# First weight sums: their loads moved to ScalarE's queue, four of five blocks' sums moved to GpSimd

## The chip, the cores and the metric

The kernel runs on one core of one Trainium2 chip. The metric is the device time of one execution in microseconds; less is better. A core has five engines, each with an instruction queue of its own that is worked through in order: TensorE (PE in the profile, with its weight loads as PEld), VectorE (DVE), ScalarE (ACT), GpSimd (POOL) and SyncE (SP). An engine's queue also issues the DMAs that are written for it; an issue that has to wait holds up what stands behind it in that queue.

## The reference

Attention with a routing mask, then a feed-forward layer with hard-swish, all in fp32:

```python
batch, n_heads, seq, head_dim = (4, 8, 768, 64);  n_clusters = 16
n_tokens, d_model, d_ff = (3072, 512, 2048)
q_assign = np.argmax(einsum('bhsd,hcd->bhsc', q_n, c_n), axis=-1)   # k_assign likewise
mask = q_assign[:, :, :, None] == k_assign[:, :, None, :]
scores = np.where(mask, scale * q @ k.T, -1e9)
attn = softmax(scores);  attn_out = attn @ v
x = attn_out.transpose(0, 2, 1, 3).reshape(B * S, H * D)
h = x @ w_in
g = h * np.clip(h + 3.0, 0.0, 6.0) / 6.0
return g @ w_out
```

## The kernel before

**Stages.** The order of the instructions is written out by hand; nothing is reordered. Heads are taken in pairs, 16 pairs in all, four to a batch.

- *Attention* (to about 240 us): the first 8 pairs, with all keys for every query. The loop runs over n, 12 steps to a pair: scores on TensorE (L400), their exponentials on ScalarE (L423), a running sum `acc` of the exponentials on GpSimd (`key_sums`, L430 and L433), the product with v on TensorE (L443). At the end of each half of a pair TensorE sums `acc` over the partitions (`pd`, L467), and VectorE takes the reciprocal (L473). Between the steps VectorE decodes the weights, which come as 8-byte numbers (L232 to L259).
- *The late pairs* (to about 790 us): the other 8 pairs are sorted by cluster first. GpSimd scatters the rows of q, k and v into DRAM by indirect DMAs (`scatter`, L1034), SyncE loads the sorted rows (`piece`, `vs`), TensorE transposes them (L919), only a band of the scores is computed, and GpSimd gathers the result back (`gather`, L1050). These steps stand in a plan of points; after each point one half of an item of the feed-forward layer follows.
- *The end*: the feed-forward layer alone.

**The feed-forward layer** is done in 12 blocks of 256 tokens, `(b, m)`. A block has 8 up items (`up`, one for two chunks of d_ff) and then 7 down items (`down`). Up items are numbered through as `u`: items 0 to 7 are block 0, 8 to 15 block 1, up to 95. Block 0 does plain products (`ph`, L607); its up items stand in the attention loop at n = 60, 64, 70, 72, 82, 84, 90 and 94. From block 1 on each item is a product of 2x2 blocks with 7 in place of 8 multiplications (`halved`), into two PSUM tiles: `uX`, whose first matmul reads `tx`, and `uY`, which reads `tx` too. `tx` holds three sums of blocks of w_in for this item, 384 KB.

**The sums.** `kept_sums(i)` makes the three sums of item i of a block by three subtractions of 128x256 (L551) and stores them in a DRAM tensor `td` (L559). During attention this is done for five of the eight i, at the up items of block 0 that `sooner` names, ahead of the item's matmuls; the other three, and a last subtraction in w_in itself, follow in the down items of block 0.

**The loads.** `first_sums(u + 2)` loads an item's sums back from `td` two items ahead, in `begin` of item u (L548). `tx` has three buffers, so the buffer of item u+2 is the one that item u-1 has read. The order in an item from block 1 on is: `begin` runs the lift of the item before on ScalarE (`raise_gates`, L499), then the load of `tx`, then the `uX` matmuls, a copy of a quarter of `uX` on ScalarE (L677) and two sums on VectorE; `end` runs `uY`, three sums on VectorE (L670), the clip of the item before (L502) and, every second item, four sums for the down products (`gated_sums`, L649, on GpSimd or VectorE).

All plain loads and stores are issued by SyncE, in the order of the program, except the load of the centroids and one store of each of the last four blocks, which ScalarE issues.

Of the kernel before, what the change touches and what calls it, by code (L numbers as in the profile page):

```python
# [12 lines left out]
ALU = mybir.AluOpType  # L13
# [106 lines left out]
def fast_path(ctx, tc, ok, q, k, v, centroids, moe_w_in, moe_w_out, out):  # L120
# [3 lines left out]
    nc = tc.nc  # L124
# [373 lines left out]
    def lift(r, h):  # L498
        nc.scalar.activation(out=r, in_=h, func=ACT.Relu, bias=half_c, scale=1.0 / 6.0)  # L499

    def clip(g, r, h):
        nc.vector.scalar_tensor_tensor(out=g, in0=r, scalar=1.0, in1=h, op0=ALU.min, op1=ALU.mult)  # L502
# [25 lines left out]
    td = dram.tile([P, HF, 3, HK, P], F32, name="td")  # L528
# [3 lines left out]
    def load_block():  # L532
        if waiting and st["free"]:
            b, m = waiting.pop(0)
            st["free"] = False
            xb = st["xb", b, m] = xbp.tile([P, NKT, 2 * P], F32, name="xb")
            nc.sync.dma_start(xb, st["xd", b][:, :, 2 * m * P : 2 * (m + 1) * P])

    def wi(s, t, i):
        f = t * HF + i  # L540
        return w_in_sb[:, s * HK : (s + 1) * HK, f * P : (f + 1) * P]

    def first_sums(u):

        blk, i = divmod(u, HF)
        if ("tx", u) not in st and 0 < blk < B * NHC:
            tx = st["tx", u] = txp.tile([P, 3, HK, P], F32, name="tx")
            nc.sync.dma_start(tx, td[:, i])  # L548

    def subtract(out_, in0, in1):  # L550
        nc.vector.tensor_tensor(out=out_, in0=in0, in1=in1, op=ALU.subtract)  # L551

    def kept_sums(i):

        tx = txp.tile([P, 3, HK, P], F32, name="tx")
        t1, t2, t4 = (tx[:, k] for k in range(3))
        for sums in ((t1, wi(0, 1, i), wi(0, 0, i)), (t2, wi(1, 1, i), t1), (t4, wi(1, 0, i), t2)):
            subtract(*sums)
        nc.sync.dma_start(td[:, i], tx)  # L559
        if i < 2:  # L560
            st["tx", HF + i] = tx
        st["kept"].add(i)

    def make_first_sums(i):
        if i not in st["kept"]:
            kept_sums(i)
        subtract(wi(0, 1, i), wi(1, 1, i), wi(0, 1, i))

    def token_sums(b, m):

# [15 lines left out]
    def ffn_items(b):  # L586
        def up(m, i):
            u = (b * NHC + m) * HF + i
            g = g_sb[:, 0:4, i]
            got = {}  # L590

            def begin():
                raise_gates()
                load_block()
                if u >= HF:
                    first_sums(u + 2)
                    halved(b, m, u, i, got)

            def end():
                if u < HF:  # L600
                    for other in sooner.get(u, ()):
                        kept_sums(other)
                    ph = psum_m.tile([P, 512], F32, name="ph", tag="m")
                    for t in range(2):
                        f = t * HF + i
                        for kt in range(NKT):
                            nc.tensor.matmul(  # L607
                                ph[:, t * HC : (t + 1) * HC], lhsT=w_in_sb[:, kt, f * P : (f + 1) * P],
                                rhs=st["xb", b, m][:, kt], start=(kt == 0), stop=(kt == NKT - 1),
                            )  # L610
                    ph = ph.rearrange("p (k c) -> p k c", k=4)
                    lift(g, ph)
                    if i < HF - 1:
                        clip(g, g, ph)
                        gated_sums(i)
                    else:
                        ending.append(lambda: (clip(g, g, ph), gated_sums(i, nc.gpsimd)))
                else:
                    got["rest"](g)
                if i == HF - 1:  # L620
                    st.pop(("xb", b, m)), st.pop(("xs", b, m), None)
                    st["free"] = True
                    load_block()

            return [begin, end]


        def raise_gates():
            for op in lifting:
                op()  # L630
            lifting.clear()
# [7 lines left out]
        def gated_sums(i, eng=None):  # L639
            if i % 2 == 0:  # L640
                return
            a11, a21, a12, a22, s1, s2, s4 = (g_sb[:, k, i - 1 : i + 1] for k in range(7))
            if eng is None:
                eng = nc.vector if st["moving"] or (i == HF - 1 and st["last"]) else nc.gpsimd
            for out_, in0, in1, op in (
                (s1, a21, a22, ALU.add), (s2, s1, a11, ALU.subtract),
                (a21, a11, a21, ALU.subtract), (s4, a12, s2, ALU.subtract),
            ):
                eng.tensor_tensor(out=out_, in0=in0, in1=in1, op=op)  # L649

        def halved(b, m, u, i, got):
            token_sums(b, m)
            tx = st.pop(("tx", u))
            xb, xs = st["xb", b, m], st["xs", b, m]
            X = psum_m.tile([P, 4, P], F32, name="uX", tag="m")

            def part(dst, w, x):
                for kt in range(HK):
                    nc.tensor.matmul(  # L659
                        dst, lhsT=w[:, kt], rhs=x(kt), start=(kt == 0), stop=(kt == HK - 1)  # L660
                    )

            def a(s, r):
                return lambda kt: xb[:, s * HK + kt, r * P : (r + 1) * P]

            def s(k):
                return lambda kt: xs[:, k, kt]

            def add(out_, in0, in1):
                nc.vector.tensor_tensor(out=out_, in0=in0, in1=in1, op=ALU.add)  # L670


            part(X[:, 0], tx[:, 1], s(1))
            part(X[:, 1], wi(0, 0, i), a(0, 0))
            part(X[:, 2], wi(0, 1, i), a(0, 1))
            sx = sxp.tile([P, 4, P], F32, name="sx")
            nc.scalar.copy(out=sx[:, 1], in_=X[:, 1])  # L677
            add(sx[:, 0], X[:, 0], sx[:, 1])
            add(sx[:, 2], X[:, 2], sx[:, 0])

            def rest(g):
                Y = st.get("psum_y", psum_m).tile([P, 4, P], F32, name="uY", tag="m")
                part(Y[:, 0], tx[:, 0], s(0))
                part(Y[:, 1], wi(1, 0, i), a(1, 0))
                part(Y[:, 2], tx[:, 2], a(1, 1))
                part(Y[:, 3], wi(1, 1, i), s(2))
                add(sx[:, 3], Y[:, 0], sx[:, 0])
                add(g[:, 3], Y[:, 0], sx[:, 2])
                add(g[:, 0:3], Y[:, 1:4], sx[:, 1:4])
                finish()  # L690
                lifting.append(lambda: lift(sx, g))
                ending.append(lambda: (clip(g, sx, g), gated_sums(i)))

            got["rest"] = rest
# [12 lines left out]
        def down(m, part):  # L707
# [30 lines left out]
            def end():  # L738
# [24 lines left out]
                if (b, m) == (0, 0):  # L763
                    for i in ([HF - 1, HF - 2], [5], [4], [], [3, 2], [0], [1])[part]:
                        make_first_sums(i)
                    if part in (0, 1):
                        weight_sums(6 + part)
                    elif part in (2, 3):
                        weight_sums(2 + part)
# [486 lines left out]
    decode = [step for i in range(NW) for step in decoding_steps(i)]  # L1256
    decode += [lambda i=i: weight_sums(i) for i in range(4)]
    st["kept"] = set()
    sooner = {0: (7,), 1: (6,), 2: (5,), 5: (4, 3)}
    up_at = (60, 64, 70, 72, 82, 84, 90, 94)  # L1260
    READY, DECODED = per_batch + 2 * lag_d, 2 * per_batch

# [411 lines left out]
@with_exitstack  # L1674
def kernel(
    ctx: ExitStack,
    tc: tile.TileContext,
    q: bass.AP,
    k: bass.AP,
    v: bass.AP,  # L1680
    centroids: bass.AP,
    moe_w_in: bass.AP,
    moe_w_out: bass.AP,
    out: bass.AP,
):
    ins = (q, k, v, centroids, moe_w_in, moe_w_out)
    flagp = ctx.enter_context(tc.tile_pool(name="flagp", bufs=1))
    ok = flagp.tile([1, 1], I32, name="ok")
    with ExitStack() as inner:
        good = fast_path(inner, tc, ok, *ins, out)  # L1690
    with tc.If(good == 0):
        with ExitStack() as inner:
            general_path(inner, tc, *ins, out)
# [32 lines left out]
```

## Time and profile before

| | |
|---|---|
| median of 3 runs | 951.38 us (949.34 to 952.5) |
| profiled execution | 952.83 us, span of its instructions 951.0 us |
| granted TensorE clock | 0.996 |
| TensorE busy | 929.3 us, 98% |
| VectorE busy | 597.0 us, 63% |
| GpSimd busy | 576.2 us, 61% |
| ScalarE busy | 349.7 us, 37% |
| loads of `tx` | 86 of 384 KB, median 3.8 us to landing |

How to read the rows of the profile: a timeline row has the start in us from the span's start, the duration in us (of a run of like instructions, with x for how many), engine, line and operation, output and inputs, and in brackets the engine's idle time before it and what ended that. `SPq` and `ACTq` are the queues of SyncE and ScalarE, mostly DMA issues; the duration of an issue is the time that it holds the queue. A row with `<-` of the waits has the total in us, how many times, and the longest. A group row has minimum, median and maximum in ns, or the busy time in us and the mean in ns. Ends of matmuls are modelled, so gaps of TensorE under some 0.15 us do not show.

### The profile page before, as it was taken

To read this page: it belongs to the slowest core of one execution; us is meant where nothing else is said; L and a number is where in the kernel's file an instruction comes from. 1 tells how busy PE (TensorE), PEld (TensorE's weight loads), DVE (VectorE), ACT (ScalarE), POOL (GpSimd) and SP (SyncE) were. 2 spreads that over 40 slices of the span, in tenths; PEclk is the share of its full clock that TensorE was granted. 3 is DMA by queue.
4 is the path that set the end of the run, shared out by engine and by line. 5 is a ranking of instruction groups with operands and counts; after the bars stand their busy time and mean duration, and the time that the engine had idled before them with its cause. 6 is when DMAs were issued, how large, how long until landed. Compare 5 with 4: busy or idle time off the path is not lost.

```text
span 951.0 us, 17617 instructions
## 1 busy us (share of the span) xinstructions
PE 929.3 (98%) x6358; PEld 726.1 (76%) x6358; DVE 597.0 (63%) x1306; ACT 349.7 (37%) x731; POOL 576.2 (61%) x1302
## 2 busy tenths in 40 slices
PE   8999999989999999999999999899999999999997
PEld 5444444555798798797897978878888799999996
DVE  6789899899976375284383573564471564636261
ACT  6888877756112232233232241241331311212120
POOL 3877767748366677787777778777777060303030
PEclk9999999999999999999999999999999999999999
DMA  7355556351364657474593654844853334323210
GB/s 200 98 134 156 133 161 175 104 154 53 95 208 136 152 150 165 129 178 118 163 226 88 156 161 129 186 146 101 199 148 83 111 85 127 91 72 106 71 52 26
DMA packets 174351, 124.23 MB, mean 131 GB/s; under 512 B 134064, under 2 KB 152496, under 8 KB 174256
## 3 DMA queue, kind: packets, MB, share of 16 engines
q1 hardware_dynamic: 164320, 109.86, 43.8%
q0 software_dynamic: 9216, 12.60, 4.7%
q8 instruction: 52, 0.85, 0.4%
q10 hardware_dynamic: 720, 0.56, 0.2%
q14 instruction: 43, 0.35, 0.1%
HBM read 94.67 MB, written 28.31 MB: 129 GB/s over the span
## 4 chain that ended last, share of the span: by engine, by line
PE 69%; DVE 3%; DMA 1%; ACT 0%; issue 0%; POOL 0%; ACTq 0%; SPq 0%
PE Y L698 18%; PE uY L659 15%; PE X L698 13%; PE uX L659 12%; PE pv L1116 3%; PE ps L1077 3%; PE ps L919 2%; PE pv L1077 1%; DMA tx<-td 1%; PE pd L1140 1%; PE pcs L337 1%; DVE g_sb L670 1%; PE ps L1157 1%; DVE g_sb L649 0%; DVE sx L670 0%; DVE g_sb L502 0%
## 5 line engine op out<-in xcount | busy, mean ns | idle before, releaser
L433 POOL TENSOR_TENSOR acc<-acc,ex 128x768 f32<-128x768 f32 x64 | 124.0, 1938 | 29.5 <-ACT ex L423 25.9
L1050 POOL DMA_INDIRECT xn<-xsd,pos x96 | 93.4, 973 | 50.5 <-ACT sx L499 28.8
L1034 POOL DMA_INDIRECT qd<-qn,pos x96 | 97.0, 1011 | 44.4 <-issue 32.7
L499 ACT ACTIVATE sx<-g_sb,half_c 128x512 f32<-128x512 f32 x88 | 63.7, 724 | 144.1 <-DVE g_sb L670 141.3
L649 POOL TENSOR_TENSOR g_sb<-g_sb 128x256 f32<-128x256 f32 x52 | 39.2, 773 | 125.2 <-DVE g_sb L502 124.2
L1034 POOL DMA_INDIRECT kvd<-kvn,pos x96 | 97.7, 1018 | 26.0 <-issue 26.0
L1026 POOL MEMSET w_low<- 128x1 f32 x864 | 91.2, 106 | 33.3
L705 DVE TENSOR_TENSOR y<-y,Y 128x256 f32<-128x256 f32 x48 | 20.2, 421 | 135.9 <-PE Y L698 132.0
L659 PE MATMUL uX<-xb,w_in_sb 128*128 128x128 f32 x704 | 93.0, 275 | 0.0
L698 PE MATMUL X<-w_out_sb,g_sb 128*128 128x256 f32 x384 | 90.6, 382 | 0.5 <-DVE g_sb L502 0.5
L698 PE MATMUL Y<-T,g_sb 128*128 128x256 f32 x384 | 88.0, 381 | 0.0
L698 PE MATMUL Y<-w_out_sb,g_sb 128*128 128x256 f32 x384 | 87.7, 380 | 0.0
L659 PEld LDWEIGHTS uX<-xb,w_in_sb 128*128 128x128 f32 x704 | 85.7, 192 | 0.0
L698 PEld LDWEIGHTS X<-w_out_sb,g_sb 128*128 128x128 f32 x384 | 70.9, 190 | 14.9 <-issue 3.9
L698 PEld LDWEIGHTS Y<-T,g_sb 128*128 128x128 f32 x384 | 72.1, 190 | 13.2 <-issue 3.9
L670 DVE TENSOR_TENSOR sx<-uX,sx 128x128 f32<-128x128 f32 x176 | 51.0, 290 | 49.3 <-ACT sx L677 45.4
L698 PEld LDWEIGHTS Y<-w_out_sb,g_sb 128*128 128x128 f32 x384 | 71.8, 190 | 10.6 <-issue 1.3
L400 PE MATMUL ps<-xf 64*128 64x384 f32 x384 | 79.3, 491 | 0.3 <-ACT ex L423 0.3
L423 ACT ACTIVATE ex<-ps 128x768 f32<-128x768 f32 x96 | 72.6, 802 | 4.5 <-PE ps L400 4.5
L443 PE MATMUL pv<-ex,vt 128*64 128x384 f32 x384 | 73.3, 503 | 0.0
L502 DVE SCALAR_TENSOR_TENSOR g_sb<-sx,g_sb 128x512 f32<-128x512 f32 x88 | 63.7, 726 | 3.1 <-ACT sx L499 3.1
L670 DVE TENSOR_TENSOR g_sb<-uY,sx 128x128 f32<-128x128 f32 (+1 forms) x176 | 65.5, 413 | 0.0
(194 smaller groups left out, 1801.2 us busy)
## 6 DMA issues: line engine op xcount, KB each, us to landing
tx<-td SPq DMA_DIRECT2D x86, 384.0 KB, 3.8
raw<-in_moe_w_in_dram SPq DMA_DIRECT2D x16, 512.0 KB, 4.6
raw<-in_moe_w_out_dram SPq DMA_DIRECT2D x16, 512.0 KB, 5.3
xb<-xd SPq DMA_DIRECT2D x12, 512.0 KB, 4.2
out_dram<-y SPq DMA_DIRECT2D x44, 128.0 KB, 1.8
qk<-in_q_dram SPq DMA_DIRECT2D x18, 192.0 KB, 5.3
qk<-in_k_dram SPq DMA_DIRECT2D x18, 192.0 KB, 4.5
vt<-in_v_dram SPq DMA_DIRECT2D x16, 192.0 KB, 3.9
```

What stands on the lines that cost most here:

```text
L400: nc.tensor.matmul(st["ps", n][:, t, 0:HALF], lhsT=x[r, NCH + j], rhs=x[r, hf * NHC : (hf + 1) * NHC], start=first, stop=last, skip_group_ ...
L423: nc.scalar.activation(out=ex, in_=sc, func=ACT.Exp, scale=SM_SCALE)
L433: nc.gpsimd.tensor_tensor(out=acc, in0=acc, in1=ex, op=ALU.add)
L443: nc.tensor.matmul(pv[t * D : (t + 1) * D], lhsT=vt[:, t, j], rhs=ex[:, t], start=(j == 0), stop=(j == NCH - 1),)
L499: nc.scalar.activation(out=r, in_=h, func=ACT.Relu, bias=half_c, scale=1.0 / 6.0)
L502: nc.vector.scalar_tensor_tensor(out=g, in0=r, scalar=1.0, in1=h, op0=ALU.min, op1=ALU.mult)
L659: nc.tensor.matmul(dst, lhsT=w[:, kt], rhs=x(kt), start=(kt == 0), stop=(kt == HK - 1))
L670: nc.vector.tensor_tensor(out=out_, in0=in0, in1=in1, op=ALU.add)
L698: nc.tensor.matmul(bank[:, half * HC : (half + 1) * HC], lhsT=g_sb[:, kind, i], rhs=w[:, i], start=(first and i == 0), stop=(last and i == ...
L1026: nc.gpsimd.memset(w_low, W_LOW)
L1034: i = nc.gpsimd.indirect_dma_start(out=rows[name, g, t], in_=src, in_offset=None, out_offset=bass.IndirectOffsetOnAxis(ap=pos[:, a, j, t : ...
L1050: nc.gpsimd.indirect_dma_start(out=xn[:, j, t], out_offset=None, in_=rows["xsd", g, t], in_offset=bass.IndirectOffsetOnAxis(ap=pos[:, 0, j ...
```

## The change

The loads of `tx` are issued by ScalarE instead of SyncE; they stand at the same place of the program. The sums made during attention are spread otherwise: before, blocks 7, 6, 5 at items 0, 1, 2 and blocks 4, 3 at item 5, all on VectorE; after, 7 at item 0, 6 at 2, 3 at 3, 5 at 4 and 4 at 6, on GpSimd at the even items and on VectorE at item 3. Their stores stay on SyncE, and what is made after attention stays on VectorE.

```diff
@@ first_sums(u)
             tx = st["tx", u] = txp.tile([P, 3, HK, P], F32, name="tx")
-            nc.sync.dma_start(tx, td[:, i])
+            nc.scalar.dma_start(tx, td[:, i])
 
-    def subtract(out_, in0, in1):
-        nc.vector.tensor_tensor(out=out_, in0=in0, in1=in1, op=ALU.subtract)
+    def subtract(eng, out_, in0, in1):
+        eng.tensor_tensor(out=out_, in0=in0, in1=in1, op=ALU.subtract)
 
-    def kept_sums(i):
+    def kept_sums(i, eng):
 ...
-            subtract(*sums)
+            subtract(eng, *sums)
         nc.sync.dma_start(td[:, i], tx)
 ...
     def make_first_sums(i):
         if i not in st["kept"]:
-            kept_sums(i)
-        subtract(wi(0, 1, i), wi(1, 1, i), wi(0, 1, i))
+            kept_sums(i, nc.vector)
+        subtract(nc.vector, wi(0, 1, i), wi(1, 1, i), wi(0, 1, i))
@@ up(m, i), end()
                 if u < HF:
-                    for other in sooner.get(u, ()):
-                        kept_sums(other)
+                    if u in sooner:
+                        kept_sums(sooner[u], nc.vector if u % 2 else nc.gpsimd)
...
-    sooner = {0: (7,), 1: (6,), 2: (5,), 5: (4, 3)}
+    sooner = {0: 7, 2: 6, 3: 3, 4: 5, 6: 4}
```

## The prediction

> **What bounds the kernel now.** I read the page first, then TensorE's own waits, then the timelines around each wait, then SyncE's queue.
>
> ```profile
> span 951.0 us, 17617 instructions
> PE 929.3 (98%) x6358; PEld 726.1 (76%) x6358; DVE 597.0 (63%) x1306; ACT 349.7 (37%) x731; POOL 576.2 (61%) x1302
> PE uX L659 <- DMA tx<-td: 3.7, 2, 2.9
> PE uX L659 <- DVE g_sb L670: 1.2, 1, 1.2
> PE X L698 <- DVE g_sb L502: 0.5, 1, 0.5
> SPq L548 <- PE uY L659: 165.1, 61, 5.7
> ```
>
> TensorE is busy for 929.3 of 951.0 us, so only time in which it idles can be won: at most 21.7 us, start and end included. The list of its waits (total us, times, longest) says what ends that idle time inside the kernel: of those the change can reach, loads of `tx` stand first, then a second wait of the same matmul, and a clip. The last line is SyncE's queue: the `tx` loads stood in it 61 times waiting for a buffer, and all that SyncE issues stood behind them. Everything else of TensorE's time is work that the change leaves alone. So I price three things: the `tx` waits, what ScalarE's queue does to the same loads, and what VectorE and GpSimd do during attention.
>
> **Part 1, the loads on ScalarE's queue: the waits removed.** The three places, in order of time:
>
> ```profile
> 262.51 2.65 SPq L559 DMA_DIRECT2D td<-tx  x2
> 268.67 0.27 ACT L677 COPY sx<-uX 128x128 f32<-128x128 f32 x1 [7.87 <-PE uX L659]
> 269.90 7.69 SPq L548 DMA_DIRECT2D tx<-td  x4
> 274.33 0.68 PE L659 MATMUL uX<-xs,tx 128*128 128x128 f32 x4 [0.79 <-DMA tx<-td]
> ...
> 544.42 0.72 ACT L499 ACTIVATE sx<-g_sb,half_c 128x512 f32<-128x512 f32 x1 [3.38 <-DVE g_sb L670]
> 547.51 0.39 SPq L548 DMA_DIRECT2D tx<-td  x1
> 552.52 0.68 PE L659 MATMUL uX<-xs,tx 128*128 128x128 f32 x4 [1.21 <-DVE g_sb L670]
> ...
> 602.32 0.98 SPq L890 DMA_DIRECT2D piece<-qd  x2
> 603.43 2.57 SPq L890 DMA_DIRECT2D piece<-kvd  x2
> 605.19 0.72 ACT L499 ACTIVATE sx<-g_sb,half_c 128x512 f32<-128x512 f32 x1 [2.82 <-DVE steps L952]
> 608.11 1.34 SPq L899 DMA_DIRECT2D qn<-in_q_dram  x2
> 609.55 0.73 SPq L548 DMA_DIRECT2D tx<-td  x1
> 614.93 0.68 PE L659 MATMUL uX<-xs,tx 128*128 128x128 f32 x4 [2.88 <-DMA tx<-td]
> tx<-td SPq DMA_DIRECT2D x86, 384.0 KB, 3.8
> DMA to landing us min/median/max: 3.3/3.8/6.6
> ```
>
> A load for item u+2 is issued in begin(u), on ScalarE right after the lift of item u-1 (L499) and ahead of the copy of item u (L677). ScalarE's place is therefore the start of that lift.
>
> Item 10: on SyncE the load comes after two output stores and the last `td` store, at 269.90. Its source was stored first in the pair that starts at 262.51, and ScalarE idles for 7.87 us up to 268.67. The load can go when that store has landed, some 267, and land by 271 at 3.8 us, ahead of the 273.54 at which TensorE was ready (274.33-0.79). Worth 0.79 us.
>
> Item 45: SyncE reached it at 547.51, ScalarE would at 544.42. With 3.8 to 6.6 us to landing it is there at 548.2 to 551.0; TensorE was ready at 552.52-1.21 = 551.31. The row blames VectorE's sum, but TensorE started 5.0 us after the load's issue, inside the range of landings, and no operand of this matmul needs that sum; I take the wait as the load's. Worth 1.21 us, or 0 if the row is right.
>
> Item 51: SyncE spent 602.32 to 609.55 on issuing pieces, `vs` and `qn` before it; ScalarE is there at 605.19. It lands at 609.0 to 611.8, and TensorE was ready at 614.93-2.88 = 612.05. Worth up to 2.88 us. Here the load joins transfers that are already queueing, and it may have to wait for earlier SyncE issues to land; I take 2.4, between 0.9 and 2.9. The sum is 0.8+1.2+2.4 = 4.4 us.
>
> **What the move adds.** The issue costs ScalarE's sequencer time, and in most items the load starts later than on SyncE, since the lift waits for VectorE:
>
> ```profile
> L709 ACTq DMA_DIRECT2D out_dram<-y x4: 339/349/358, 797.8 to 945.5; - x4
> 799.85 0.61 PE L659 MATMUL uX<-xs,tx 128*128 128x128 f32 x4
> 801.10 0.72 ACT L499 ACTIVATE sx<-g_sb,half_c 128x512 f32<-128x512 f32 x1 [2.57 <-DVE g_sb L670]
> 801.73 0.24 ACT L677 COPY sx<-uX 128x128 f32<-128x128 f32 x1
> 806.11 0.61 PE L659 MATMUL uX<-xs,tx 128*128 128x128 f32 x4
> ...
> 280.65 0.61 PE L659 MATMUL uX<-xs,tx 128*128 128x128 f32 x4
> 282.68 0.72 ACT L499 ACTIVATE sx<-g_sb,half_c 128x512 f32<-128x512 f32 x1 [3.03 <-DVE g_sb L670]
> 286.91 0.61 PE L659 MATMUL uX<-xs,tx 128*128 128x128 f32 x4
> ```
>
> An issue on ScalarE takes 0.35 us (four stores). 86 of them are 30 us of a sequencer whose engine is 37% busy. In seven of eight items the issue falls under the running lift (0.72 us), so the copy behind it need not move: cost 0. If it doesn't overlap, the copy comes 0.35 to 0.4 us later, and behind the copy stand VectorE's two sums of the item; the bank that they free is wanted two items later, so TensorE doesn't see it alone.
>
> The delay counts more. In the packed items (799.85) the lift starts 1.25 us after the item; the load is needed at 806.11, 6.26 us after the item's start. 6.26-1.25-0.1-3.8 leaves 1.1 us. On SyncE it left 2.4. So nothing is lost at the median landing. The tightest place is 280.65: the lift is 2.03 us late there, which leaves 6.26-2.03-0.1-3.8 = 0.3 us; at the longest landing of 6.6 us it would be 2.5 us late. The four loads from 269.90 held SyncE for 7.69 us; what stands behind them now goes up to that much earlier, which thins the crowd here. I take 0.5 us of loss, between 0 and 2.5.
>
> **Part 2, the sums on GpSimd.** Each block's sums are three subtractions and a store.
>
> ```profile
> 138.05 2.19 POOL L430 TENSOR_TENSOR acc<-ex 128x768 f32<-128x768 f32 x1 [1.42 <-ACT ex L423]
> 138.50 2.03 DVE L551 TENSOR_TENSOR tx<-w_in_sb 128x256 f32<-128x256 f32 x1
> 140.56 0.88 DVE L551 TENSOR_TENSOR tx<-w_in_sb,tx 128x256 f32<-128x256 f32 x2
> 144.06 4.04 POOL L433 TENSOR_TENSOR acc<-acc,ex 128x768 f32<-128x768 f32 x2 [3.81 <-ACT ex L423]
> 174.23 1.82 POOL L430 TENSOR_TENSOR acc<-ex 128x768 f32<-128x768 f32 x1 [4.38 <-ACT ex L423]
> 209.93 1.81 POOL L430 TENSOR_TENSOR acc<-ex 128x768 f32<-128x768 f32 x1 [6.19 <-ACT ex L423]
> 230.29 8.53 POOL L433 TENSOR_TENSOR acc<-acc,ex 128x768 f32<-128x768 f32 x4 [2.71 <-ACT ex L423]
> 240.20 0.81 PE L467 MATMUL pd<-acc,ones 128*64 128x384 f32 x4
> L649 POOL TENSOR_TENSOR g_sb<-g_sb x16: 721/728/1704, 156.0 to 249.8; 128x256 f32<-128x256 f32 x16
> 212.43 0.69 ACT L499 ACTIVATE g_sb<-ph,half_c 128x512 f32<-128x512 f32 x1 [1.73 <-PE ph L607]
> 213.65 0.68 DVE L502 SCALAR_TENSOR_TENSOR g_sb<-g_sb,ph 128x512 f32<-128x512 f32 x1
> ```
>
> GpSimd does the same shape in 0.73 us (L649), so a block costs it 3 x 0.73 = 2.2 us. The four blocks are queued behind the steps at n = 60, 70, 82 and 90, where TensorE works on the up item and no new exponentials come: GpSimd idles 3.81, 4.38, 6.19 and 2.71 us just there. 2.2 fits in each; behind it stand the running sums `acc`, and behind those the denominators. Cost 0; if an instruction is held up as the 1.70 us one was, the last gap overflows by 0.5 us, which the 1.4 us between the end of the last `acc` (230.29+8.53 = 238.82) and its matmul at 240.20 still cover. The stores stay on SyncE but wait for GpSimd, about 1 us longer; raw weights, loaded two chunks ahead, are queued behind them.
>
> A sum on VectorE beside GpSimd's addition took 2.03 us, alone 0.44 (0.88 for two): the two exclude each other. Moving it therefore doesn't end the exclusion, it only turns it round. VectorE gets back 2.9 us at n = 60, but its next operation, the clip, had to wait for the lift anyway. The block that stays, at n = 72, goes ahead of the next clip, which waits for a lift in the same way. At n = 84 two blocks go: the clip ran at 213.65, the lift was done at 213.12, so VectorE gains 0.5 us and hands it on to the clip for which TensorE waits 0.5 at the end of attention. I take 0.4, between -0.5 and 0.5.
>
> [...]
>
> **Sum.** -4.4 +0.5 -0.4 = -4.3 us. The profiled execution took 952.83 us (span 951.0), 1.45 above the median of the three runs, 951.38. Its sum is 948.5; from the median, 947.1.
>
> **The rivals.**
>
> Crowding: item 45's and item 51's loads land late because the 16 DMA engines are full, not because SyncE was late. For it: some landing took 6.6 us, and SyncE's issues from 602.32 on stretch to over 1 us each, as if they pushed into a full queue. Against it: from issue to start item 51's took 614.93-609.55 = 5.4 us, so 605.19 still gives 610.6, ahead of 612.05. Then only item 10's 0.8 us and 0.4 of part 2 stay, less 0.5: 950.7, no change that can be told. Chance 0.22. [...]
>
> Landing on ScalarE's queue, slower: where items follow each other without other work, PE, VectorE, the lift and the load now form a ring over two items: 1.25+0.1+landing+0.1. It decides from a landing of 4.8 us on, above 3.8 but below 6.6, the longest now. The packed stretches are items 11 to 15, 70 to 71, and the last three blocks, some 25 items. At 6.0 us the ring takes 7.45 instead of 6.26, 0.6 us an item, 15 us in all: 951.4-4.3+15 = 962. At 5.3 it is 0.25 an item, 6 us: 953. It also happens if an SyncE issue that hangs keeps ScalarE's next issue waiting. Against it: in the last blocks few other transfers run. Chance 0.18.
>
> **How the numbers follow.** About 0.3% (2.85 us) is what a measurement of this kernel can tell. The forecast, 944.5 to 948.5, has 0.60: all of it faster. Its best sum, 0.79+1.21+2.88+0.5 with nothing lost at 280, is 5.4 us and gives 946.0; the three runs reach 2.0 below their median, and 1.5 of that is kept below. Its worst, 0.8+1.2+0.9 saved, gives 948.5. Crowding gives same, 0.22; the ring slower, 0.18. The range for 8 in 10 runs from 944.5 to 953.
>
> **What would show it.** Right: the wait of uX for `tx` gone at items 10, 45 and 51, the issues in ScalarE's records 0.35 us long and inside the lift, SyncE's 165 us of waiting for uY gone, GpSimd's L551 at 0.73 us inside the four gaps, attention ending within 0.5 us of now. Wrong: new waits of uX for `tx` in items 11 to 15 or 75 to 95, `tx` landings over 4.8 us, or matmuls of the denominators waiting for `acc`.

## The result, and the profile after

The changed kernel took 949.09 us (median of 22 runs, 946.99 to 952.76) against 951.44 us before (22 runs, 949.34 to 953.98): ratio 0.9979, 95% interval 0.997 to 0.9989, or 2.35 us. Run again on another occasion it took 949.35 us against 954.13: ratio 0.9953 (0.9936 to 0.9969). Faster, as forecast, but by 2.35 us where 4.3 were forecast: 949.09 us lies above the forecast's 944.5 to 948.5. The two ratios' intervals do not meet, so the ratio also hangs on the occasion.

The profiled execution took 947.94 us. Its page, the list of TensorE's waits (total, times, longest) and the line of the loads:

```profile
span 946.1 us, 17635 instructions
PE 928.3 (98%) x6358; PEld 726.5 (77%) x6358; DVE 591.6 (63%) x1294; ACT 349.5 (37%) x731; POOL 583.9 (62%) x1314
PE po L379 <- DVE one_hot L357: 2.5, 2, 2.3
PE uX L659 <- DMA tx<-td: 2.0, 1, 2.0
PE X L698 <- DVE g_sb L502: 0.4, 1, 0.4
PE X L698 <- POOL g_sb L649: 0.2, 1, 0.2
tx<-td ACTq DMA_DIRECT2D x86, 384.0 KB, 3.5
```

The three waits of before are gone, and so is SyncE's waiting for uY at L548. But a wait for `tx` is still there, once, of 2.0 us: it is a new one. First the three places, in the timeline of the changed kernel (start, duration):

```profile
265.65 0.34 ACTq L548 DMA_DIRECT2D tx<-td  x1
272.59 0.61 PE L659 MATMUL uX<-xs,tx 128*128 128x128 f32 x4
...
544.74 0.33 ACTq L548 DMA_DIRECT2D tx<-td  x1
551.37 0.61 PE L659 MATMUL uX<-xs,tx 128*128 128x128 f32 x4
...
604.07 0.33 ACTq L548 DMA_DIRECT2D tx<-td  x1
610.67 0.61 PE L659 MATMUL uX<-xs,tx 128*128 128x128 f32 x4
```

None of the three matmuls (items 10, 45, 51) has a bracket any more. Set beside before, TensorE gains 0.95, 1.38 and 3.04 us there, 5.37 in all. Item 38 gives 2.17 back. Here is the same place, first before the change, then after it; the last line is of SyncE's waits after:

```profile
478.78 0.32 SPq L548 DMA_DIRECT2D tx<-td  x1
479.19 0.98 SPq L890 DMA_DIRECT2D piece<-qd  x2
480.26 2.25 SPq L890 DMA_DIRECT2D piece<-kvd  x2
482.48 0.61 PE L659 MATMUL uX<-xs,tx 128*128 128x128 f32 x4
485.61 0.61 PE L659 MATMUL uX<-xs,tx 128*128 128x128 f32 x4
...
469.60 6.00 SPq L890 DMA_DIRECT2D piece<-qd  x2
475.70 1.43 SPq L890 DMA_DIRECT2D piece<-kvd  x2
478.53 0.72 ACT L499 ACTIVATE sx<-g_sb,half_c 128x512 f32<-128x512 f32 x1 [2.57 <-DVE g_sb L670]
480.74 0.61 PE L659 MATMUL uX<-xs,tx 128*128 128x128 f32 x4
481.24 0.33 ACTq L548 DMA_DIRECT2D tx<-td  x1
481.67 0.27 ACT L677 COPY sx<-uX 128x128 f32<-128x128 f32 x1 [2.42 <-DMA piece<-kvd]
486.04 0.68 PE L659 MATMUL uX<-xs,tx 128*128 128x128 f32 x4 [2.00 <-DMA tx<-td]
SPq L890 <- DMA qd<-qn,pos: 15.5, 4, 6.6
```

Items 37 and 38 start 3.13 us apart before (482.48 and 485.61) and 5.30 after (480.74 and 486.04). After, the lift starts at 478.53, and the issue of the load should stand 0.1 us behind it, as 48 of the 86 loads of this execution stand behind the lift ahead of them. It stands at 481.24, and the copy behind it names a transfer that ScalarE's work does not read: `piece<-kvd`. The traces of before and after have a completion semaphore with each of the 403 DMAs that SyncE and ScalarE issue: eight semaphores, 100 to 107, with 50 or 51 DMAs each, taken in turn (in before's SyncE queue 394 of 397 issues take the number after that of the issue ahead; ScalarE issues five there). In both traces all 395 issues that follow another on their semaphore leave behind the last landing that is recorded for that other one. In before none comes closer behind it than 0.54 us; after, three come within 0.08, and each follows a DMA of the other queue: at 0.02 us (SyncE's `kvn<-in_k_dram` at 608.62), 0.06 and 0.08 (ScalarE's load at 540.84). The one at 0.06 is the load of item 38. It is the 235th DMA, the second `piece<-kvd` the 227th, both on semaphore 102, and that one lands at 481.18. I read this as ScalarE's issue waiting for SyncE's DMA to land, and call it the hold.

Eleven profiled executions of this and the later runs have the load of item 38 held in this way. In nine the issue comes 0.06 or 0.07 us behind that landing; in the other two the trace lacks part of the landing's records. The load then takes 4.7 us to land. Issued at 478.6 it would, at the same 4.7 us, have landed at 483.3, before TensorE was ready at 484.04; how long it would have taken is an estimate (in `pause2` below, issued at 478.59, it took 5.4).

Before, the load stood ahead of the pieces in SyncE's own queue. Now SyncE no longer spends its time on loads of `tx`: it comes to the pieces at 469.60 instead of 479.19, has to wait there for GpSimd's scatter, and the load of item 38 comes eight places behind the second `piece<-kvd`. The places are those of the compiled program; why it has the pieces ahead of the load is not shown. Before, the line of SyncE's waits read:

```profile
SPq L890 <- DMA qd<-qn,pos: 4.4, 1, 4.4
```

Two differences between the two profiled executions are not the change's. The start is 0.99 us longer after. And before has a stretch of half clock that the changed kernel's execution hasn't, though both have the same wait for `one_hot`. The view by stretches shows it (stretch, its length, busy us of each engine, granted clock, DMA share, GB/s), first before, then after:

```profile
192.00:196.00 4.00, 1.74 (x18) 0.80 (x16) 3.86 (x8) 0.13 (x1) 3.45 (x2) 1.00 0.75 203
196.00:200.00 4.00, 4.00 (x18) 1.65 (x16) 3.88 (x4) 3.94 (x11) 0.16 (x1) 0.57 1.12 259
...
194.00:198.00 4.00, 1.75 (x18) 1.16 (x18) 3.86 (x8) 1.21 (x2) 2.38 (x2) 1.00 1.03 272
198.00:202.00 4.00, 4.00 (x22) 2.41 (x19) 3.91 (x3) 3.27 (x10) 1.23 (x1) 1.00 1.15 283
```

It lasted 3.41 us and cost 1.65. TensorE's end moved by -4.33 us (the span by -4.9): +0.99 (start) -1.65 (half clock) -5.37 +2.17, and -0.5 in small steps. What makes the small steps was not followed. Without the first two the change made -3.7 us in this pair.

Part 2 did what it says and little for the time:

```profile
L551 POOL TENSOR_TENSOR tx<-w_in_sb,tx x8: 724/730/1061, 142.0 to 228.4; 128x256 f32<-128x256 f32 x8
L551 POOL TENSOR_TENSOR tx<-w_in_sb x4: 724/726/1184, 141.2 to 226.3; 128x256 f32<-128x256 f32 x4
```

0.73 us an instruction (minimum, median, maximum in ns), as forecast. Between 200 and 241 us TensorE's marks keep their distance to before within 0.05 us; the clip's wait is 0.4 for 0.5.

### The profile page after: what moved, and what is told of

It is laid out like the page before. It is cut to its first block, busy times and chain, and to the rows that moved or that the text cites. A ratio compares the mean times of both kernels' runs of the same rounds, so it can differ in the third digit from the quotient of the medians.

```text
span 946.1 us, 17635 instructions
## 1 busy us (share of the span) xinstructions
PE 928.3 (98%) x6358; PEld 726.5 (77%) x6358; DVE 591.6 (63%) x1294; ACT 349.5 (37%) x731; POOL 583.9 (62%) x1314
## 4 chain that ended last, share of the span: by engine, by line
PE 70%; DVE 2%; DMA 1%; ACT 0%; POOL 0%; issue 0%; SPq 0%; ACTq 0%
PE Y L698 18%; PE uY L659 15%; PE X L698 13%; PE uX L659 12%; PE pv L1116 3%; PE ps L1077 3%; PE ps L919 2%; PE pv L1077 1%; PE pd L1140 1%; PE pcs L337 1%; PE ps L1157 1%; DMA piece<-kvd 1%; DVE g_sb L649 0%; DVE g_sb L502 0%; DVE g_sb L670 0%; DVE sx L670 0%
```

## The experiments

Each kernel is compared with the kernel before on the same chip and occasion. Between occasions before's median moved from 951.4 to 954.1, so ratios of different occasions are set side by side with care.

**The two halves, the whole again, and the load further ahead.** `act_only` is before with one line of the change:

```diff
-            nc.sync.dma_start(tx, td[:, i])
+            nc.scalar.dma_start(tx, td[:, i])
```

> Only the loads of tx go to ScalarE's queue; the sums are as before the change. Theory A: 949.0 to 949.7 us, the whole gain of about 2.3 us, with the wait of about 2 us near 485. Theory C (the sums on GpSimd make half of the gain or more, by freeing VectorE in attention): 950.2 us or more.

`pool_only` is the changed kernel with this line undone.

> Only the sums are spread as in the change; the loads of tx stay in SyncE's queue. Theory A: 951.0 to 951.7 us, no difference, and waits of uX for tx near 274, 551 and 611 as before. Theory C: 950.2 us or less, with attention ending over 0.5 us sooner.

`after_again` is the changed kernel unaltered.

> The changed kernel once more, for a second profile of the same program. Theory A (the loads' move makes the gain, and part of it is given back at one place, where ScalarE's issue of the load of item 38 is held by the landing of a piece that SyncE issued late): 948.6 to 949.6 us, waits of uX for tx none near 274, 551 and 611, one of about 2.0 us near 485. Theory B (the waits for tx are chance of one execution, since landings vary): the same median, but the wait near 485 is gone or elsewhere, or others of over 0.5 us appear in items 11 to 15 or 75 to 95.

`load_first` is the changed kernel with the load at the head of begin(u), ahead of the previous item's lift:

```diff
             def begin():
+                if u >= HF:
+                    first_sums(u + 2)
                 raise_gates()
                 load_block()
                 if u >= HF:
-                    first_sums(u + 2)
                     halved(b, m, u, i, got)
```

> The changed kernel with the load of tx ahead of the lift in begin, so that ScalarE's queue issues it as soon as its buffer is read and does not wait for VectorE: some 1.2 us earlier in most items. Theory A: the later issue costs nothing as landings are below 4.8 us, so 948.6 to 949.6 us as the changed kernel, and the wait near 485 stays, since it hangs on the piece's landing. Rival (the ring of lift, load and product is what took back the gain): over 1 us faster than the changed kernel, 948 us or less.

Measured against 954.13 us before: act_only 954.71 (12 runs), ratio 1.0004 (0.9988 to 1.0019); pool_only 953.09, 0.999 (0.998 to 1.0001); after_again 0.9953; load_first 947.95, 0.9934 (0.9917 to 0.9952). So the theory that the loads bring the whole gain by themselves fell as it was written: alone they bring none in the median. The sums alone bring 0.1%, and the interval does not exclude that they bring nothing; pool_only's profile keeps the three waits of before (0.63, 0.44 and 1.83 us). after_again has none of these three and loses 1.83 us at item 38, as theory A said; but it also waits 0.48, 0.71 and 0.72 us for `tx` at items 11, 13 and 44, as theory B said, 3.6 us in four waits. So some of the losses vary from one execution to the next.

Yet act_only's profiled execution, 951.27 us, is second fastest of its twelve, and its TensorE lost the same waits as the changed kernel's (-0.95, -1.2, -3.04) and gave back 2.63 us at item 38 and 1.6 at item 13.

load_first's median is where the rival put it (948 us or less), and theory A was wrong that the wait at item 38 stays: the profile has no wait that is put down to `tx`, and item 38 follows item 37 by 3.13 us, the undisturbed distance. The load is issued at 478.27, ahead of the lift, and eight places ahead of it stands the load of item 36, which left at 470.84; so this is no proof of the rival's ring, since the hold is gone as well. Its six runs can't be told from after_again's (the intervals overlap). Its profiled execution (952.21 us, the slowest of six) lost some 4.3 us against after_again's at 672 to 679: 2.7 us in which TensorE and ScalarE stood still together for a reason that the trace doesn't give, and 1.6 us by half clock behind it.

**Once more, the engine or the places, the pieces later, the scatter quicker.** `act_twice` is act_only again.

> The kernel before with the loads of tx on ScalarE and nothing else: the same program as act_only, run a second time. In act_only its profiled execution (951.27 us) lost three waits of before and won two others, -1.65 us at TensorE's end, but the median of its 12 runs was 1.0004 of before. Theory D (the sums' part matters to the loads' part): again 0.9985 to 1.002, and a profile in which a load of tx is late at places where the changed kernel has none, 3 us or more in all. Theory E (the earlier median was chance of an occasion): 0.995 to 0.998, as the changed kernel.

`sums_on_dve`:

```diff
-                        kept_sums(sooner[u], nc.vector if u % 2 else nc.gpsimd)
+                        kept_sums(sooner[u], nc.vector)
```

> The changed kernel with all five blocks' sums made by VectorE, at the changed kernel's places (one block a step); loads of tx on ScalarE as there. It differs from act_only in the places of the sums alone, from the changed kernel in the engine alone. Theory D1 (it is the engine: GpSimd takes work from VectorE): as act_only, near 1.000 of before. Theory D2 (it is the places: which block is summed in which step): as the changed kernel, 0.995 to 0.998. Theory E (only the loads count): also 0.995 to 0.998, and act_twice with it.

`queries_later`:

```diff
-                (-36, cluster_scores), (-34, own_clusters), (-33, run_up), (-32, step_up), (-32, load_queries),
+                (-36, cluster_scores), (-34, own_clusters), (-33, run_up), (-32, step_up), (-30, load_queries),
```

> The changed kernel with the loads of the sorted queries' pieces two steps later in the work beside the items (-30 for -32), so that other DMAs stand eight places ahead of the loads of tx of items 36 to 39, 44 to 47 and so on. Theory A (a load of tx on ScalarE is held until the DMA eight places back has landed; at item 38 that costs 2.0 us): the hold of about 2 us at 479 goes or moves; 0.997 to 0.999 of the changed kernel if no other takes its place, and up to 1.003 if the pieces' own consumers now wait. Rival (the load is late because DMA engines are full): the wait at item 38 stays within 0.5 us.

`pause2`:

```diff
-    PAUSE = 3
+    PAUSE = 2
```

> The changed kernel with two waiting instructions of GpSimd between indirect DMAs for three, so that the scatter of sorted rows ends some 5 to 10 us sooner for each step of 24 and the pieces that wait for it are issued sooner. Theory A: the load of tx for item 38 is not held, and the 2.0 us wait there goes; 0.996 to 0.999 of the changed kernel. Rival (crowding: what decides is how many DMAs run at once): the quicker scatter crowds the other loads, waits for tx grow by 1 us or more elsewhere, 1.000 to 1.004 of the changed kernel.

Measured against 951.81 us: act_twice 951.82, 0.9998 (0.9985 to 1.001); sums_on_dve 951.23, 0.9989 (0.9976 to 1.0002); queries_later 949.41, 0.9976 (0.9964 to 0.9988); pause2 946.69 (945.89 to 947.62), 0.9949 (0.9931 to 0.9967). act_only's flat median was no chance. sums_on_dve lies between theories D1 and D2 and decides neither. queries_later did not do what it was meant to: eight places ahead of the load now stands the first `piece<-kvd` in place of the second, and the load is still held, by 1.4 us. Item 38 loses 1.2 us instead of 2.2, and the time can't be told from the changed kernel's first ratio. In pause2 the hold is gone. Its time is clear of the changed kernel's first ratio, not of its second (0.9936 to 0.9969). Its timeline at the same place:

```profile
469.55 0.97 SPq L890 DMA_DIRECT2D piece<-qd  x2
471.55 0.95 SPq L890 DMA_DIRECT2D piece<-kvd  x2
478.59 0.33 ACTq L548 DMA_DIRECT2D tx<-td  x1
480.70 0.61 PE L659 MATMUL uX<-xs,tx 128*128 128x128 f32 x4
484.14 0.68 PE L659 MATMUL uX<-xs,tx 128*128 128x128 f32 x4 [0.15 <-DMA tx<-td]
```

The two `piece<-qd` take 0.97 us of SyncE instead of 6.00, `piece<-kvd` goes 4 us sooner, and the load leaves 2.11 us before item 37 starts, where it left 0.50 us behind that start with the hold. Of the 2.0 us wait 0.15 is left. The rival had a little right too: the load took 5.4 us to land, and item 44 now waits 0.61 us for `tx`.

**Is it the hold, and what does half clock add?** `act_pause2` is act_only with `PAUSE = 2`, `before_pause2` is before with it. Their expectations, in this order:

> act_only (loads of tx on ScalarE, all sums on VectorE as before) with two waiting instructions of GpSimd for three. act_only and act_twice stood level with the kernel before, although their profiled executions lost 4 us of waits; their runs lie 2 to 4 us above the profiled one and at a lower mean clock. Theory G (the gate: a wait of TensorE of 2.2 to 2.6 us, as at item 38, brings in some executions a stretch of 3.4 us at half clock, 1.7 us, which eats the gain): without the wait at item 38 the mean clock is 0.997 to 0.999 in most runs and the time 0.995 to 0.997 of before, as pause2. Theory D1 (GpSimd's sums are worth 0.3% by themselves): 0.998 to 1.000 of before, 0.3% above pause2.

> The kernel before with two waiting instructions of GpSimd for three, and nothing of the change. Theory A (the quicker scatter gains only where it frees a load of tx that stands in a queue behind it): before's loads of tx stand on SyncE's queue behind the issues of pieces that wait for the scatter, so some of its waits at items 45 and 51 shrink: 0.997 to 1.000 of before. Rival (the quicker scatter is a gain of its own, of 0.25% or more, whatever queue the loads are on): 0.997 or less, and then pause2 owes it nothing of the hold.

`decode_later` is the changed kernel with the step that makes `one_hot` further ahead:

```diff
+        if 72 <= n < 84:
+            return {0: 6, 2: 4, 4: 2, 6: 3, 8: 5, 10: 8}[r]
         if n < DECODED - per_pair:
```

> The changed kernel with decode steps between step 72 and 84 of the attention put elsewhere, so that VectorE makes the one_hot for which TensorE waits 2.3 us near 192.6 us sooner. Theory G: that wait goes (2.3 us) and with it the stretch of half clock that follows it in part of the executions (1.7 us): 2 to 4 us, 0.996 to 0.998 of the changed kernel, 0.992 to 0.995 of before, and mean clocks of 0.998 to 0.999 in most runs. Rival (the wait only moves to the next decode): 0.999 to 1.002 of the changed kernel.

`three` puts three of the edits together:

> The changed kernel with three edits of earlier runs together: the load of tx issued ahead of the lift (load_first), two waiting instructions of GpSimd for three (pause2), decode steps between 72 and 84 put elsewhere (decode_later). If the losses are separate (late loads, the hold at item 38, the wait for one_hot with the half clock behind it) they add up: 943 us at most, 0.990 to 0.992 of before, with nearly all runs at a mean clock of 0.998 or 0.999. If the edits get in each other's way (the hold only moves), not below 0.994.

Measured against 952.12 us: act_pause2 947.93, 0.9951 (0.9939 to 0.9964); before_pause2 952.29, 0.9997 (0.9989 to 1.0006); decode_later 947.28, 0.995 (0.9936 to 0.9964); three 944.36 (943.82 to 945.02), 0.9918 (0.9905 to 0.993).

The first two settle the place of the loss. The quicker scatter does nothing for a kernel whose loads are on SyncE, whose waits it leaves standing:

```profile
PE uX L659 <- DMA tx<-td: 4.2, 3, 2.4
PE po L379 <- DVE one_hot L357: 2.5, 2, 2.2
```

and it gives act_only the whole 0.5% that act_only lacked (0.9951, where it had 1.0004 and 0.9998). With the hold out of the way no difference can be told by who makes the sums (0.9951 and 0.9949). The hold is not the whole wait at item 38, though. In act_pause2's profile the load leaves 0.10 us behind the lift and still comes late:

```profile
480.19 0.33 ACTq L548 DMA_DIRECT2D tx<-td  x1
486.63 0.68 PE L659 MATMUL uX<-xs,tx 128*128 128x128 f32 x4 [1.04 <-DVE steps L952]
```

It took 6.3 us to land, at a place where the DMA engines are busy (in the changed kernel DMA share 1.18 from 480 to 484 us, against 0.26 in its last blocks, 806 to 846). So crowding may well cost something at item 38 besides the hold; no run tests it.

decode_later took the 2.3 us wait for `one_hot` out; some 0.5 us of it came back as a longer wait for a clip (1.0 us for 0.4). Its 0.995 of before is at the edge of what theory G said, and can't be told from the changed kernel's second ratio; the changed kernel itself was not run on that occasion. `three`, with this edit and the other two, has neither of the two waits of 2 us left; of its `one_hot` line remains

```profile
PE po L379 <- DVE one_hot L357: 0.3, 1, 0.3
```

It beats both kernels (its interval lies below both of the changed kernel's), by 7.8 us the one before; the 943 us that the expectation allowed at most it missed by 1.4. Its five runs lie within 1.2 us at mean clocks of 0.998 and 0.999; the changed kernel's 22 lay within 5.8 us, ten of them at 0.993 to 0.996.

**More executions of the two, with a profile.** `act_look1`, `act_look2` and `act_look3` are act_only again, `after_look` is the changed kernel again.

> Another execution of act_only (loads of tx on ScalarE, sums as before), looked at alone. Theory G: 946 to 949 us where every wait of TensorE stays under 2.2 us, 950 to 953 us with stretches of half clock right behind the waits for one_hot (193), item 38 (485) or another load of tx. Theory W (no clock: the waits themselves are longer in most executions than in the two profiled ones): 951 to 956 us at a mean clock of 0.998 or 0.999, with waits of 2 us or more on tx at items that had none.

> As act_look1, a further execution: 946 to 949 us without and 950 to 953 us with stretches of half clock behind waits (theory G); 951 to 956 us at full clock with longer waits on tx (theory W).

> As act_look1, a further execution: 946 to 949 us without and 950 to 953 us with stretches of half clock behind waits (theory G); 951 to 956 us at full clock with longer waits on tx (theory W).

> Another execution of the changed kernel. Theory A: the wait at item 38 is again 1.8 to 2.2 us, and 946 to 948 us if no stretch of half clock follows it, 948 to 950 us if one does. Theory W: other waits on tx of 1 us or more.

Measured: 951.71, 951.23, 949.57 and 948.18 us (before: 952.26). In act_look1 the wait at item 38 is the longest of all, and half clock follows; its timeline, then the view by stretches:

```profile
481.03 0.61 PE L659 MATMUL uX<-xs,tx 128*128 128x128 f32 x4
481.74 0.34 ACTq L548 DMA_DIRECT2D tx<-td  x1
487.81 0.78 PE L659 MATMUL uX<-xs,tx 128*128 128x128 f32 x4 [3.49 <-DVE steps L952]
...
484.00:488.00 4.00, 0.51 (x5) 0.34 (x4) 3.79 (x14) 0.87 (x2) 2.89 (x10) 1.00 1.10 286
488.00:492.00 4.00, 4.00 (x27) 3.93 (x27) 2.71 (x9) 1.32 (x3) 3.39 (x9) 0.57 0.80 199
```

The row blames VectorE's `steps`, which this matmul doesn't read; the load was issued 0.71 us after item 37 and took 5.9 us to land. act_look2 is alike (2.97 us more than undisturbed, then half clock); act_look3 and after_look have the wait (2.2 and 2.7 us) and full clock. So theory G's half clock is there in two of act_only's three. The waits are longer as well, but at item 38, not at the items that had none, as theory W would have it.

In the traces of before and after the granted clock changes on the marks of a grid. In before's it stays at 1.0 for 191.15 us, at 0.5 for 3.413 (from 196.56 on) and at 1.0 for 747.52: 56, 1 and 219 times 3.413 us. After the change it stays at 1.0 for 935.25 us, 274 times. Set against this grid of windows of 3.41 us, the executions sort themselves. The busy share is the share of a window in which TensorE was busy. For the waits that left TensorE busy for less than 0.46 of a window inside the kernel, and for item 38 in the changed kernel's three, the share and what followed:

| execution | place | busy share | half clock in the next window |
|---|---|---|---|
| act_look1 | item 38 | 0.13 | yes |
| act_look2 | item 38 | 0.22 | yes |
| before_pause2 | item 51 | 0.29 | yes |
| pool_only | one_hot | 0.34 | yes |
| before | one_hot | 0.36 | yes |
| load_first | 673 us | 0.38 | yes |
| act_pause2 | one_hot | 0.40 | yes |
| before | item 51 | 0.43 | no |
| sums_on_dve | one_hot | 0.43 | no |
| after_again | one_hot | 0.44 | no |
| after_look | item 38 | 0.44 | no |
| decode_later | item 38 | 0.45 | yes |
| act_only | item 38 | 0.45 | no |
| after_again | item 38 | 0.51 | no |
| after | item 38 | 0.63 | no |

In these executions a wait of 2.2 us or more brought half clock when it fell nearly whole into one window (busy share of 0.40 or less, seven of seven), and not when it was cut by the edge of one (0.43 to 0.45, none of five). The wait for `one_hot` is the same 2.2 to 2.3 us everywhere it stands, and has half clock behind it in 3 of 16 profiled executions. From 0.43 to 0.45 the share alone does not decide.

## Why the prediction was right and wrong

**Part 1, the waits removed: right, a little small.** 4.4 us were forecast, 5.37 came: 0.95 for 0.8, 1.38 for 1.2, 3.04 for 2.4. Item 45's wait was the load's, though its row named VectorE. The rival of crowding fell for these two: items 45 and 51 gave their waits up, and the median landing went from 3.8 to 3.5 us. It did not fall everywhere: the loads of item 38 took 4.7 to 6.3 us to land in the kernels that have them on ScalarE behind the lift. What the change of issuer saved was not small beside a landing of 3.5 us: the load of item 51 left at 604.07 where it left at 609.55, with TensorE only 1.2 us ahead by then, because it no longer stood behind the pieces.

**What the move adds: the step that failed.** "I take 0.5 us of loss, between 0 and 2.5." In three executions of the changed kernel one item alone, item 38, lost 2.17, 1.83 and 2.66 us. The slack was worked out from the lift and the landing alone, 0.3 to 1.1 us. What was left out is a third term, the DMA eight places ahead, which kept ScalarE's issue 2.6 us behind its place. The rival mentioned an issue of SyncE that keeps ScalarE's next waiting, but priced it as a ring over 25 items. In the changed kernel's trace it costs TensorE time at one. The slack itself held in the last blocks, which have no wait for `tx` in these three executions. In the packed items 11 to 15 it held in two of the three. In after_again item 11's load landed late, the lift behind item 11 started 2.94 us after that item instead of 1.25, since VectorE was late as well, and item 13 waited too, 1.2 us for both. So what the second rival feared did happen there for two items; at item 14 it was over. With item 44's, that execution has 3.6 us of waits for `tx`, beyond the 2.5 of the range.

**What was not in the sum at all** is that half clock behind a wait of some 2 us adds to the loss: 1.65 us behind the 2.26 us wait in before, some 1.6 behind 2.41 us in before_pause2 (item 51) and behind 1.87 us in decode_later (item 38). It stood in the trace of before, at 196.6, where 1.65 us of the 952.83 came from it. So before pays it too: on the occasion of pause2 its runs at a clock of 0.998 or 0.999 took 949.7 to 950.8 us, those at 0.995 953.2 to 954.1. For act_only it is shown at item 38 in two of five executions. For the changed kernel it wasn't seen there in three; that its runs at a mean clock of 0.996 or less owe their 1 to 5 us to it is an inference from those clocks. The waits alone, -5.4 and +2.2, would make a gain of 3.2 us; how much of the way from there to the median's 2.35 is half clock, and how much waits like after_again's, stays open.

**Part 2: 0.4 us forecast, under 0.1 found in attention.** The gaps took the sums, as forecast. But as long as the hold is there, the sums' part may matter: act_only stayed level with before where the changed kernel gained 0.2 to 0.5%; and sums_on_dve stood between, 0.9989. Item 38 lost 2.63, 2.25, 3.65, 2.97 and 2.18 us in act_only's five executions, a mean of 2.7 against the changed kernel's 2.2, with two stretches of half clock. On its first occasion act_only had runs of 953.7 to 955.6 us at a clock of 0.999 as well, which half clock doesn't explain. Why the hold is longer there stays open.

## What to carry to other kernels

A transfer moved to another queue leaves the line that it stood in (item 51's load left 5.48 us sooner), but what stood behind it now arrives sooner, and may wait where it never did (SyncE came to the pieces at 469.60 for 479.19, and its two `piece<-qd` took 6.00 us for 0.98); look for the wait that the early arrival makes, and for whoever shares its completion semaphore. Price a wait of the busiest engine by what follows it as well. And where a row blames a tile that the waiting instruction doesn't read, take the operand that landed last.

## What the runs showed of the hardware

Two issuing queues with no common buffer were coupled by the eight semaphores that their DMAs take in turn. In the changed kernel's trace 395 of 395 issues left behind the recorded landing of the DMA before them on their semaphore, three of them within 0.08 us of a landing of the other queue's; at item 38 ScalarE stood for 2.4 us for a transfer of SyncE's, and with a quicker producer of that transfer (`pause2`) the load left at 478.59 for 481.24. That edit took the kernel with loads on ScalarE from 1.0004 and 0.9998 to 0.9951 of before, and left before, in whose trace no issue comes within 0.54 us of such a landing, at 0.9997.

The changes of TensorE's granted clock lie on a grid of 3413 ns in both traces: 56, 1 and 219 steps apart in before's, 274 in the changed kernel's. In the executions of the table half clock came for one window after each of the seven windows in which TensorE was busy for 0.40 or less; at 0.43 to 0.45 it came once in six, behind a wait of 1.87 us (decode_later at 484, share 0.45).
